# Moving the third and fourth output store of each batch from ScalarE's queue to SyncE's

## The chip, the cores and the metric

The kernel runs on one core of a Trainium2 chip. The time is device microseconds of a whole execution; lower is better. A profiled execution also gives a span from the first to the last instruction, some 1.7 us less than the time. Ratios are the mean time of one kernel's fast runs over that of the other's of the same rounds, so they are not quite the ratio of the medians that are quoted; a run is called slow when it is over 1.5% above the fastest of the same kernel. "First scores" below is the start of a batch's first score matmul, and a batch is measured from its first scores to the next batch's.

## The reference

Causal attention with 16 extra "beacon" keys that every query sees, then a gated feed-forward block:

```python
scores = q @ concat(beacon_k, k).T / 8          # B, H, S, D = 8, 8, 576, 64
scores = where(causal, -1e9, scores)
x = softmax(scores) @ concat(beacon_v, v)       # -> 4608 tokens x 512
out = (gelu(x @ w_gate) * (x @ w_val)) @ w_out  # d_ff = 1536, result float32
```

## The kernel before

A pass of the batch loop (b = 1 to 7) does, interleaved on TensorE, the output matmuls of feed-forward chunk b-1 (`o(n)` issues n of 48), the scores and attention of batch b, and then the gate and value matmuls of chunk b. The output leaves in four stores of 256 KB each. Attention outputs are turned by DMA transposes on SyncE (`turn_dma`), and so are the q and k of batch b+1 (`transpose_dma`, ten of them). GpSimd issues the loads of batch b+2.

```python
def store(engine):
    for out_ap, in_ap in stores:
        keep(engine.dma_start(out=out_ap, in_=in_ap))
    stores.clear()
...
            turn_dma(b, 2)
            o(6)
            av(b, 3)
            o(7)
            store(nc.scalar)          # third store of the batch
            turn(b, 3)
            put(b, 3)
            o(4)
            keep(nc.scalar.preload_act_table_set(SET_GELU))
            for kk in (0, 3, 1, 2):
                for fi in range(2):
                    gv_mms(b, fi, kk, last=kk == 2)     # Gelus 0 and 1
        for fi in range(F_TILES):
            if fi >= 2:
                gate_val(b, fi, ...)                    # matmuls, Gelu, product
            ...
            if fi == 0:
                store(nc.scalar)      # fourth store: behind Gelus 0 and 1 on ScalarE
                if b and b + 1 < B:
                    hold(b, 2)
                    load_v(b + 1)
                if b and b + 2 < B:
                    load_qk(b + 2)
                if 2 <= b + 1 < B:
                    transpose_dma(b + 1)
```

Three PSUM buffers (the pool `psum_s`) are shared by the scores and by the gate and value results.

The softmax here doesn't subtract the row's maximum and nothing guards it: scores larger than these inputs give would overflow.

## Time and profile before

| | before |
|---|---|
| time, first three runs | 372.77, 375.12, 615.39 us (the last a lone outlier) |
| profiled span, mean granted TensorE clock | 371.4 us, 0.999 |
| TensorE, ScalarE busy | 361.0, 187.1 us |
| stores on ScalarE, on SyncE | 28 of 256 KB, 9 (the last two chunks) |

The page, the waits, one batch of the timeline and the windows batch by batch are shown and read in the prediction. In the waits, a line is "who waits, for whom: us in total, times, longest". In the timeline, a line is start, length, engine, source line, operation, operands, and in brackets the idle time just before it with what ended it; SPq and ACTq are instructions that only issue a DMA. In the windows, a line is the stretch, its length, then busy time (and instruction count) of TensorE's matmuls and weight loads, VectorE, ScalarE and GpSimd, then granted clock, DMA share and GB/s.

### The profile page before, as it was taken

How to read it: one execution, taken by the hardware profiler on the slowest of the kernel's cores; microseconds unless marked ns; L12 is line 12 of the kernel's file. 1: busy time of each engine (PE TensorE's matmuls, PEld its weight loads, DVE VectorE, ACT ScalarE, POOL GpSimd, SP SyncE). 2: the span in 40 equal slices, each digit the busy share in tenths (PEclk: the TensorE clock that was granted, in tenths of full speed). 3: DMA queues.
4: the chain of work that ended last, by engine and by line, in shares of the span. 5: the costliest groups of instructions: out<-in, count | busy, mean ns of one | idle time of the engine just before them, and what ended most of it. 6: DMA issues, size and time to landing. Idle time of an engine off the chain costs nothing.

```text
span 371.4 us, 7554 instructions
## 1 busy us (share of the span) xinstructions
PE 361.0 (97%) x3061; PEld 182.6 (49%) x3061; DVE 151.5 (41%) x277; ACT 187.1 (50%) x243; POOL 160.5 (43%) x288
## 2 busy tenths in 40 slices
PE   7899999999998999999989999999999999999996
PEld 6664446444643455444634454445534464444443
DVE  4554545332533334433524253434444353424332
ACT  3963587238823593349623882369324963331210
POOL 8834486574548152944384453835320430000000
PEclk9999999999999999999999999999999999999999
DMA  8999999899179924999399936992491040000103
GB/s 109 178 204 205 192 131 145 103 158 139 50 114 170 125 66 92 142 152 75 98 120 148 124 52 111 174 128 75 94 165 30 28 112 29 0 2 28 56 34 111
DMA packets 154900, 39.65 MB, mean 107 GB/s; under 512 B 141424, under 2 KB 150384, under 8 KB 154864
## 3 DMA queue, kind: packets, MB, share of 16 engines
q0 software_dynamic: 104848, 19.11, 72.1%
q1 hardware_dynamic: 45984, 12.71, 21.7%
q10 hardware_dynamic: 4032, 7.34, 6.3%
q8 instruction: 24, 0.39, 0.5%
q14 instruction: 12, 0.10, 0.1%
HBM read 38.27 MB, written 9.44 MB: 128 GB/s over the span
## 4 chain that ended last, share of the span: by engine, by line
PE 85%; DMA 5%; SPq 4%; DVE 3%; ACT 1%; issue 1%; ACTq 0%
PE gv_ps L172 38%; PE o_ps L172 24%; PE x_ps L172 9%; PE s_ps L172 8%; DMA qkT<-q_sb 5%; SPq L238 3%; PE t_ps L180 2%; PE v_ps L172 2%; PE g_ps L172 2%; DVE qkT L217 1%; PE w_ps L172 1%; SPq L368 1%; DVE hT_sb L427 1%; DVE y_sb L336 1%; ACT ge_sb L175 1%
## 5 line engine op out<-in xcount | busy, mean ns | idle before, releaser
L175 ACT ACTIVATE ge_sb<-gv_ps 128x512 bf16<-128x512 f32 x101 | 58.5, 597 | 139.3 <-PE gv_ps L172 124.3
L427 DVE TENSOR_TENSOR hT_sb<-gv_ps,ge_sb 128x512 bf16<-128x512 f32 x101 | 68.2, 690 | 120.7 <-ACT ge_sb L175 120.6
L172 PE MATMUL gv_ps<-xT_sb,wg_sb 128*128 128x512 bf16 x404 | 111.6, 379 | 3.5 <-DVE hT_sb L427 3.5
L172 PE MATMUL gv_ps<-xT_sb,wv_sb 128*128 128x512 bf16 x404 | 111.5, 379 | 0.0
L172 PE MATMUL o_ps<-wo_sb,hT_sb 128*128 128x512 bf16 (+2 forms) x444 | 106.7, 374 | 0.0
L175 ACT ACTIVATE expT<-s_ps 128x960 bf16<-128x960 f32 (+3 forms) x112 | 99.7, 967 | 7.9 <-PE s_ps L172 7.5
L298 POOL TENSOR_SCALAR_AFFINE_SELECT expT<-expT 128x256 bf16<-128x256 bf16 (+2 forms) x140 | 51.5, 385 | 65.5 <-ACT expT L175 64.9
L172 PEld LDWEIGHTS <-wg_sb 128*128 128x128 bf16 x432 | 42.0, 98 | 54.8 <-issue 4.9
L172 PEld LDWEIGHTS <-wv_sb 128*128 128x128 bf16 x432 | 42.2, 98 | 50.5
L172 PEld LDWEIGHTS <-hT_sb 128*128 128x128 bf16 x444 | 38.8, 97 | 42.3 <-DVE y_sb L336 3.1
L172 PEld LDWEIGHTS <-expT 128*128 128x128 bf16 (+1 forms) x960 | 33.5, 97 | 11.0 <-DVE y_sb L336 4.3
L172 PE MATMUL x_ps<-v_sb,expT 128*128 128x65 bf16 (+1 forms) x960 | 37.1, 193 | 0.0
L108 POOL DMA_DIRECT2D v_sb<-in_v_dram x40 | 33.7, 860 | 5.9 <-DMA wv_sb<-in_moe_w_val_dram 1.7
L172 PE MATMUL s_ps<-qkT 64*128 64x512 bf16 (+5 forms) x384 | 33.5, 281 | 2.5 <-DVE qkT L221 1.6
L446 DVE COPY o_sb<-o_ps 128x512 f32<-128x512 f32 (+2 forms) x37 | 25.0, 676 | 26.6 <-PE o_ps L172 25.4
L108 POOL DMA_DIRECT2D k_sb<-in_k_dram x30 | 25.2, 842 | 20.0 <-DMA q_sb<-in_q_dram 13.6
L336 DVE TENSOR_TENSOR y_sb<-x_ps,r_sb 128x320 bf16<-128x320 f32 (+1 forms) x47 | 28.8, 612 | 1.6
L334 DVE RECIPROCAL r_sb<-x_ps 128x5 f32<-128x5 f32 (+1 forms) x47 | 9.6, 204 | 47.1 <-PE x_ps L172 47.1
L108 POOL DMA_DIRECT2D q_sb<-in_q_dram x30 | 25.4, 885 | 4.4 <-DMA wo_sb<-in_moe_w_out_dram 3.5
L172 PEld LDWEIGHTS <-qkT 64*128 64x128 bf16 x384 | 14.3, 94 | 19.3 <-issue 11.0
L378 POOL COPY hold_sb<-xT_sb 128x2 bf16<-128x2 bf16 x6 | 1.1, 185 | 34.1 <-DMA xT_sb<-y_sb 34.1
L613 ACT ACT_TABLE_LOAD x7 | 9.0, 1283 | 10.8 <-DVE o_sb L446 10.8
(49 smaller groups left out, 118.8 us busy)
## 6 DMA issues: line engine op xcount, KB each, us to landing
out_dram<-o_sb ACTq DMA_DIRECT2D x28, 256.0 KB, 3.0
v_sb<-in_v_dram POOLq DMA_DIRECT2D x24, 128.0 KB, 6.4
q_sb<-in_q_dram POOLq DMA_DIRECT2D x24, 128.0 KB, 9.2
k_sb<-in_k_dram POOLq DMA_DIRECT2D x18, 128.0 KB, 7.7
out_dram<-o_sb SPq DMA_DIRECT2D x7, 256.0 KB, 2.0
wo_sb<-in_moe_w_out_dram POOLq DMA_DIRECT2D x3, 512.0 KB, 14.4
wg_sb<-in_moe_w_gate_dram POOLq DMA_DIRECT2D x2, 512.0 KB, 11.1
wv_sb<-in_moe_w_val_dram POOLq DMA_DIRECT2D x2, 512.0 KB, 12.7
```

The lines of the kernel that those rows point to most:

```text
L108: keep(nc.gpsimd.dma_start(out=out_ap, in_=in_ap))
L172: keep(nc.tensor.matmul(out_ap, lhsT, rhs, start=start, stop=stop, **kw))
L175: keep(nc.scalar.activation(out_ap, in_ap, func, **kw))
L180: keep(nc.tensor.transpose(out_ap, in_ap, ident[0:n, 0:n]))
L217: keep(nc.vector.tensor_copy(out_ap, in_ap))
L238: nc.sync.dma_start_transpose(out=qkT[:, :, w, c + j * P : c + j * P + n], in_=src[0:n, j, :, :].rearrange("p h d -> p (h d)"),)
L298: nc.gpsimd.affine_select(out=d, in_=d, pattern=[[0, 2], [1, n]], compare_op=ALU.is_ge, fill=0.0, base=NB if t == 0 else 0, channel_multip ...
L334: keep(nc.vector.reciprocal(r, x[:, :, :, D:DV]))
L336: nc.vector.tensor_tensor(out=y_of[i][:, :, h0:h1, :].rearrange("p j b d -> p b j d"), in0=x[:, :, :, 0:D], in1=r.to_broadcast([P, h1 - h0 ...
L427: nc.vector.tensor_tensor(out=h_of[ci][:, fi, :], in0=gv_of.pop((ci, fi))[1], in1=ge_sb, op=ALU.mult)
L446: keep(nc.vector.tensor_copy(o_sb[:, ti, c0:c1], o_ps))
L613: keep(nc.scalar.preload_act_table_set(SET_GELU))
```

## The change

The third and fourth store of each batch are issued on SyncE's queue again, behind the turns. The intent is to free ScalarE's queue.

```diff
             av(b, 3)
             o(7)
-            store(nc.scalar)
+            store(nc.sync)
             turn(b, 3)
...
             if fi == 0:
-                store(nc.scalar)
+                store(nc.sync)
                 if b and b + 1 < B:
                     hold(b, 2)
```

## The prediction

> **What bounds the kernel now.** I read the page first, then the waits, then one batch of the timeline, then the batches side by side.
>
> ```profile
> span 371.4 us, 7554 instructions
> PE 361.0 (97%) x3061; PEld 182.6 (49%) x3061; DVE 151.5 (41%) x277; ACT 187.1 (50%) x243; POOL 160.5 (43%) x288
> ...
> PE 85%; DMA 5%; SPq 4%; DVE 3%; ACT 1%; issue 1%; ACTq 0%
> ...
> out_dram<-o_sb ACTq DMA_DIRECT2D x28, 256.0 KB, 3.0
> ```
>
> TensorE is busy for 361.0 of 371.4 us, so no change that leaves its work alone can win more than 10.4 us (2.8%), and some of that is the start. ScalarE is half idle: taking 14 of its 28 store issues away (0.34 us each in the trace, 4.8 us in all) is worth nothing as work. What counts is where a store on ScalarE's in-order queue waits. The table of waits shows it:
>
> ```profile
> ACT ge_sb L175 <- DMA qkT<-q_sb: 14.9, 4, 4.4
> ...
> ACT L613 <- DVE o_sb L446: 10.8, 7, 1.6
> ...
> PE gv_ps L172 <- DVE hT_sb L427: 3.5, 4, 1.4
> ```
>
> A Gelu has no reason to wait for a DMA transpose of the next batch's q. The timeline of the second pass of the batch loop (b = 2) explains it; these are rows of it:
>
> ```profile
> 102.08 0.37 ACTq L454 DMA_DIRECT2D out_dram<-o_sb  x1
> ...
> 105.17 0.69 DVE L446 COPY o_sb<-o_ps 128x512 f32<-128x512 f32 x1 [0.41 <-PE o_ps L172]
> ...
> 105.66 1.21 SPq L238 DMA_TRANSPOSE qkT<-q_sb  x1
> ...
> 108.26 1.22 SPq L238 DMA_TRANSPOSE qkT<-q_sb  x1
> ...
> 113.31 0.34 ACTq L454 DMA_DIRECT2D out_dram<-o_sb  x1
> ...
> 113.75 1.57 ACT L175 ACTIVATE ge_sb<-gv_ps 128x512 bf16<-128x512 f32 x3 [4.42 <-DMA qkT<-q_sb]
> ...
> 115.12 1.02 PE L172 MATMUL gv_ps<-xT_sb,wg_sb 128*128 128x512 bf16 x4 [1.36 <-DVE hT_sb L427]
> ```
>
> The fourth store's data were copied by 105.86, but it issues only at 113.31. In the built program it waits on two semaphores: VectorE's, and one of eight that the hardware DMAs take in turn. The earlier user of that one is the second q transpose, issued at 108.26, landed at 113.23. Behind the store stand the Gelus; they come late, VectorE's product comes late, no score buffer is free, and TensorE stands for 1.36 us. Now the batches side by side, in windows from one batch's first output matmul to the next's:
>
> ```profile
> 86.53:127.37 40.84, 39.48 (x319) 19.42 (x317) 16.08 (x29) 21.90 (x29) 21.50 (x39) 1.00 1.30 116
> 127.37:166.83 39.46, 39.46 (x318) 19.43 (x317) 16.17 (x29) 22.00 (x29) 21.22 (x38) 1.00 1.21 115
> 166.83:207.42 40.59, 39.48 (x318) 19.43 (x317) 16.08 (x29) 21.89 (x29) 21.21 (x38) 1.00 1.30 113
> 207.42:247.06 39.64, 39.48 (x319) 19.40 (x317) 16.14 (x29) 22.01 (x29) 21.22 (x38) 1.00 1.26 116
> ```
>
> The second column is the length, the third TensorE's busy time. The work is 39.47 us each time; batches 2 and 4 (and 6) are over a microsecond longer than 3 and 5. The four idle gaps before such Gelu-released matmuls are 1.36 (b=2), 1.11 (b=4), 0.16 (b=5) and 0.91 us (b=6): 3.54 us. This is what the change can win.
>
> **What the Trainium skill says.** "DMA: Bandwidth & Descriptors", section "Issuing engines are not separate DMA queues": DMAs started by ScalarE, SyncE or GpSimd run on the same 16 engines and interleave, so the choice of issuer saves only the issuer's own time. The trace agrees for the bytes, but the cost here is a wait in the issuer's queue (4.4 us), not the 0.34 us of issuing. The same page, "Queues, rings and completion order": SP and ACT each have one ring on each engine, descriptors are consumed in ring order, and an engine takes packets from its rows in rotation. So stores put ahead of transposes in SyncE's ring hold those back, while in ScalarE's ring they shared. In the trace before, SyncE's transposes land in the order of issue, which fits; a store between transposes in that ring is not seen. "Perfetto Trace Analysis", section "DMA Instruction — HWDGE (DVE, Sync)": the profiled window of such a DMA starts once its semaphores are satisfied and leaves out the data movement. The case agrees: the blocked store shows 0.34 us, and its 7.4 us of waiting show only as others' idle time.
>
> **The change, part by part.** TensorE, VectorE and GpSimd keep their instruction lists exactly; ScalarE loses 14 DMAs (two for each of b = 1 to 7), SyncE gains them, both placed after the six turn transposes of the batch and before the ten transposes of the next.
>
> 1. Store three leaves ScalarE, which now waits 1.5 us for it before the table load (10.8 us over seven). ScalarE next works when a first gate matmul group is done (108.25, over 4 us after the load ends). Worth 0.
>
> 2. Store four leaves ScalarE. Its wait goes, so the 3.54 us of TensorE idle go: -3.54. In the new program the two stores wait on semaphores of DMAs eight places earlier, long landed by then, and no Gelu stands behind them.
>
> 3. SyncE's transposes start later. In b = 2 SyncE ends its last turn at 105.56 and starts the first q at 105.66. Now it issues store three (0.34, ready since 102.05) and store four (0.34, data ready at 105.86): estimated 105.65 to 106.41, so q moves to about 106.5: +0.85 us. In odd batches SyncE is free earlier (b = 3: 145.36, copy ends 146.69), so it waits for the copy: q at about 147.15 instead of 145.47, +1.7; but that q issue took 1.98 us instead of the usual 1.21, and if this slow issue does not recur just later, the second transpose moves by 0.9 only.
>
> 4. The stores' bytes change place. One store's packets took 13 us of engine time (6.3% of 16 x 371.4 us over 28 stores), 0.83 us on all 16. Before, store four moved in the midst of the GpSimd loads and the transposes (landed 119.90, and for that microsecond the transposes' ring moved almost nothing). Now it moves near 107, before those loads' packets begin (109). That gives the last transposes back about 0.85. Store three moves from an idle time into one with few transposes: no more than what item 3 counted.
>
> Net for the last transpose's landing: even batches about 0 to +0.4, odd 0 to +0.9. What does it cost? The next batch's scores need the last k transpose about 1.4 us after their batch starts (four output matmuls, 0.86, and some 0.5 into the first scores). Slack before: 1.0 (b=1: landed 86.89, batch at 86.53), 1.3 (b=2: 127.43, 127.37), 0.7 (b=3: 167.50, 166.83), 1.6 (b=4: 207.16, 207.42), 0.2 (b=5: 248.21, 247.06), and 7 in b=6, where no loads run (281.69, 287.44). Removing the stall brings the scores forward by just that stall, so the slack left is 1.0, 0, 0.7, 0.5, 0 and 6. I charge 0.3 in b = 2 and 0.5 in b = 5, and 0.2 over the rest: +1.0 of new waits at the scores.
>
> Sum: -3.54 + 1.0 = -2.5 us on the profiled execution.
>
> **Rivals.** (a) The transposes become the bound. For: slack is nearly nothing in b = 2 and 5, and the last transposes land 7 to 9 us after issue, so a late start sits in front of a crowded stretch. If the delay at the end were 2 us in each of b = 1 to 5, the waits would be 1 + 2 + 1.3 + 1.5 + 2 = 7.8 and the time 4.3 us longer, about 377.5. Against: the last four transposes are limited by shared DMA engines, from which store four is taken away. (b) A free win: if transposes land no later at all, the whole 3.5 us come, about 369.5. For it: b = 6 surely wins its 0.91. (c) Nothing: the waits at the scores eat just what the Gelu stall gave, since both hang on the same DMA engines; 373. I hold this for likelier than (a). (d) Mixing plain copies with transposes in a ring slows the transposes' issue; some issues take 2.0 to 2.5 us already, for a reason the profile does not show. Two more of those in each of six batches would delay as in (a).
>
> **Range and chances.** The three timed runs are 372.77, 375.12 and an outlier of 615.39; the profiled run was 373.12. I take 373.2 as what an undisturbed run gives, not the median. 373.2 - 2.5 = 370.7, and I add 0.5 because medians of few runs lie above the quiet ones: 371.2. Low end 368.8 (all of 3.5 won, and a little), high end 376.5 (most of rival a, or a disturbed median). Over 2% faster would need 7.5 us below 375.12, twice the idle time that the change can reach: 0.03. Over 2% slower needs rival (a) at twice my worst case: 0.03.
>
> **What would show it.** Right: no ScalarE wait on the q transposes; TensorE's idle before the Gelu-released matmuls gone; batches 2, 4 and 6 near 39.5 us; the first q of each batch at SyncE 0.8 to 1.7 us later against the last turn; the last k transposes landing within 1 us of where they did from the batch's start. Wrong: TensorE or its weight loads waiting for the k transposes by over 1 us in several batches (item 4 failed), or a stall that stays although the store has gone (item 2 failed), for instance because the Gelus wait for something that the store's wait hid.

## The result

The changed kernel takes 368.98 us (median of four, 368.65 to 369.70); before, 374.05 in the same comparison, or 372.77 to 375.12 without the outlier. The ratio of the fast runs is 0.9878 (0.9832 to 0.9925): 1.2% less. The profiled span fell from 371.4 to 367.4 us. The page of the changed kernel (span; busy time by engine; the chain that ended last; issues of the stores with size and us to landing):

```profile
span 367.4 us, 7507 instructions
...
PE 356.8 (97%) x3018; PEld 182.4 (50%) x3061; DVE 152.4 (41%) x277; ACT 188.3 (51%) x243; POOL 160.7 (44%) x288
...
PE 74%; DMA 13%; SPq 4%; POOL 3%; issue 2%; DVE 2%; ACT 1%; POOLq 0%; DVEq 0%
...
out_dram<-o_sb SPq DMA_DIRECT2D x21, 256.0 KB, 2.4
out_dram<-o_sb ACTq DMA_DIRECT2D x14, 256.0 KB, 2.8
```

TensorE's busy time is no measure of the gain: 43 matmul records are missing from this trace. The chain runs more through DMA here (13% against 5%), but that is no sign of a new bound: in the two repeats below the share is 2% and 7%. The waits of the changed kernel:

```profile
ACT ge_sb L175 <- PE gv_ps L172: 143.1, 89, 6.5
...
PEld L172 <- DMA qkT<-k_sb: 1.6, 4, 0.4
...
PEld L172 <- DMA xT_sb<-y_sb: 1.5, 3, 0.8
```

The 14.9 us that Gelus waited for q transposes, and TensorE's 3.5 us behind them, are no longer in the table; Gelus wait for matmuls only. What is left on TensorE are small waits for k transposes and for turns. The same stretch of the timeline (b = 2):

```profile
104.77 1.00 SPq L454 DMA_DIRECT2D out_dram<-o_sb  x2
105.87 1.21 SPq L238 DMA_TRANSPOSE qkT<-q_sb  x1
...
107.55 1.08 ACT L175 ACTIVATE ge_sb<-gv_ps 128x512 bf16<-128x512 f32 x2 [6.01 <-PE gv_ps L172]
...
109.70 0.60 ACT L175 ACTIVATE ge_sb<-gv_ps 128x512 bf16<-128x512 f32 x1 [1.07 <-PE gv_ps L172]
```

Both stores go out on SyncE in one go, and the third Gelu starts 1.07 us after the second ends, with its matmuls, instead of 4.42 us after it. And the batches side by side, b = 2 to 5:

```profile
85.83:125.14 39.31, 38.94 (x314) 19.48 (x317) 16.27 (x29) 22.11 (x29) 21.24 (x38) 1.00 1.22 115
125.14:165.16 40.02, 39.20 (x314) 19.41 (x317) 16.27 (x29) 22.12 (x29) 20.50 (x37) 1.00 1.23 115
165.16:204.48 39.32, 38.95 (x314) 19.57 (x317) 16.27 (x29) 22.11 (x29) 21.98 (x39) 1.00 1.30 116
204.48:244.13 39.65, 39.19 (x314) 19.44 (x317) 16.27 (x29) 22.11 (x29) 21.24 (x38) 1.00 1.22 120
```

A batch without any wait is 39.32 us, not 39.47. The long batches before (2, 4) are at that floor; batches 3 and 5 have new waits. From the two traces, first scores to first scores:

| us | start | b=1 | b=2 | b=3 | b=4 | b=5 | b=6 | rest |
|---|---|---|---|---|---|---|---|---|
| before | 46.90 | 40.42 | 40.84 | 39.46 | 40.59 | 39.64 | 40.38 | 83.17 |
| after | 46.37 | 40.26 | 39.32 | 40.02 | 39.32 | 39.65 | 39.32 | 83.18 |

Batches 2 and 4 gain 2.79 us, batch 6 gains 1.06, batch 3 loses 0.56. The 0.53 us at the start is chance: in another profile of the changed kernel the start is 46.87.

### The profile page after: what moved, and what is told of

Same layout as the page of the kernel before. It is cut to its first block, busy times and chain, and to the rows that moved or that the text cites.

```text
span 367.4 us, 7507 instructions
## 1 busy us (share of the span) xinstructions
PE 356.8 (97%) x3018; PEld 182.4 (50%) x3061; DVE 152.4 (41%) x277; ACT 188.3 (51%) x243; POOL 160.7 (44%) x288
## 2 busy tenths in 40 slices
DMA packets 154900, 39.65 MB, mean 108 GB/s; under 512 B 141424, under 2 KB 150384, under 8 KB 154864
## 4 chain that ended last, share of the span: by engine, by line
PE 74%; DMA 13%; SPq 4%; POOL 3%; issue 2%; DVE 2%; ACT 1%; POOLq 0%; DVEq 0%
PE gv_ps L172 32%; PE o_ps L172 23%; PE x_ps L172 9%; PE s_ps L172 7%; DMA qkT<-k_sb 7%; DMA q_sb<-in_q_dram 4%; SPq L238 3%; DMA qk<-in_q_dram 2%; POOL v_sb L108 2%; DMA xT_sb<-y_sb 1%; PE v_ps L172 1%; ACT expT L175 1%; PE t_ps L180 1%; PE g_ps L172 1%; POOL qk L108 1%
## 5 line engine op out<-in xcount | busy, mean ns | idle before, releaser
L175 ACT ACTIVATE ge_sb<-gv_ps 128x512 bf16<-128x512 f32 x101 | 59.5, 597 | 145.1 <-PE gv_ps L172 143.1
L427 DVE TENSOR_TENSOR hT_sb<-gv_ps,ge_sb 128x512 bf16<-128x512 f32 x101 | 69.1, 691 | 116.0 <-ACT ge_sb L175 116.0
L172 PE MATMUL o_ps<-wo_sb,hT_sb 128*128 128x512 bf16 (+2 forms) x415 | 101.7, 373 | 1.4 <-issue 0.2
```

The lines of the kernel that those rows point to most:

```text
L172: keep(nc.tensor.matmul(out_ap, lhsT, rhs, start=start, stop=stop, **kw))
L175: keep(nc.scalar.activation(out_ap, in_ap, func, **kw))
L427: nc.vector.tensor_tensor(out=h_of[ci][:, fi, :], in0=gv_of.pop((ci, fi))[1], in1=ge_sb, op=ALU.mult)
```

## The experiments

Theory **W**: the gain is the end of one wait. On ScalarE, Gelus stand behind the fourth store, and that store waits for the semaphore that a q transpose of the next batch used before it. What is lost again comes from transposes that now start later. Rival **Q**: ScalarE's queue is relieved of issues and of waits for copies, third store as much as fourth. Rival **T**: the bytes leave the crowded stretch and go ahead of it. All kernels below gave correct results.

**The changed kernel again** (run twice), as a yardstick.

> The changed kernel again, as the yardstick on this chip for the three others: about 369.0 us, ratio to before about 0.988 (seen: 0.9878), profiled span 367.4 within 0.5.

> The changed kernel once more beside the next three: 368.6 to 369.4 us, ratio to before 0.988.

Measured: 369.36 us, ratio 0.9883 (0.9842 to 0.9924), and 369.58 us, ratio 0.9883 (0.9852 to 0.9913). The place of the new waits changes: batch 3 was 39.31 and batch 5 39.96 us in the first of these profiles, 39.72 and 39.91 in the second. Their sum over b = 2 to 6, above 39.32, is 0.6 to 1.0 us in the three profiles.

**Only the fourth store on SyncE.**

```diff
             if fi == 0:
-                store(nc.scalar)
+                store(nc.sync)
```

> Only the fourth store goes to SyncE; the third stays on ScalarE with its 1.5 us wait before the table load. Theory W (the gain is the end of the Gelus' wait behind the fourth store's DMA semaphore): all of the gain, 369.0 us or up to 0.5 less because SyncE has one issue less ahead of the transposes; no Gelu waits for a q transpose. Rival Q (the gain is ScalarE's queue being relieved, third store as much as fourth): about half of the gain, 371 us. Rival T (bytes moved out of the crowded stretch): also about 369.

Measured: 369.52 us, ratio 0.9888 (0.9844 to 0.9932). All the gain is there with the third store, and its 1.5 us wait before the table load, still on ScalarE. Q would have had half. W holds, though the median is half a microsecond above its 368.5 to 369.0: in the profile no Gelu waits for a q transpose, and batches 2 to 6 are 39.32 us long but for one of 39.62. (That profiled run, 371.11 us, lost some 2 us at its start, in 6.83 us at half the clock.) T is not touched.

**Only the third store on SyncE.**

```diff
             o(7)
-            store(nc.scalar)
+            store(nc.sync)
             turn(b, 3)
```

> Only the third store goes to SyncE, ahead of the transposes; the fourth stays on ScalarE behind the second Gelu, and the built program still has it wait for the second q transpose. Theory W (the gain is the end of that wait): no gain; the transpose starts some 0.4 us later, so the stalls stay or grow a little: 373 to 375 us. Rival Q (ScalarE's queue relieved): half of the gain, 371.

Measured: 382.12 us, ratio 1.0202 (1.0119 to 1.0284), slower, by more than W said; whether it is slower by over 2% is unclear. Its profile (a slow execution at granted clock 0.991; the fast ones had 0.991 and 0.995) shows where:

```profile
ACT ge_sb L175 <- DMA qkT<-q_sb: 21.3, 4, 5.6
...
PE gv_ps L172 <- DVE hT_sb L427: 12.6, 6, 2.6
```

Now all six batches b = 1 to 6 stall. This run gives a scale. With t the issue of the fourth store after the batch's first scores, and the idle time of TensorE that follows (b = 1 is left out: its batch has other work in it, 40.26 us without a stall against 39.32):

| | b=2 | b=3 | b=4 | b=5 | b=6 |
|---|---|---|---|---|---|
| before: t, idle | 25.98, 1.36 | 24.61, 0 | 25.74, 1.11 | 24.77, 0.16 | 25.53, 0.91 |
| third only: t, idle | 26.81, 2.19 | 26.36, 2.03 | 26.13, 1.50 | 26.68, 2.06 | 27.19, 2.57 |

In eight of the nine stalls, idle is t - 24.62 within 0.01 us (26.36 is the exception, by 0.29). TensorE pays for each microsecond by which that store is late, one for one; W's reading is that this begins once the three result buffers are full. The store was later because the transpose it waits for was: SyncE did the third store first. W missed two things. It allowed 0.4 us for this delay, but after the first scores the second q transpose was issued 0.1 to 1.3 us later than before and landed 0.4 to 3.2 us later, so the idle time grew from 3.5 to 12.6 us. And in two stretches of 3.41 us after a stall the granted clock was 0.5.

**The fourth store ahead of the table load and of all Gelus, on ScalarE.** Bytes, copy and the semaphore waited for are unchanged.

```diff
             o(4)
+            store(nc.scalar)
             keep(nc.scalar.preload_act_table_set(SET_GELU))
```

> The fourth store on ScalarE is moved ahead of the table load and the first Gelus; its bytes, semaphore and copy are the same, and it still waits for the second q transpose. W: now all Gelus stand behind it, and with three score buffers TensorE stops after the third gate/value group: some 5 to 6 us more idle in each of batches 1 to 6 than with no wait, so 395 to 405 us. Q and rival T (bytes and their time decide): no change, 373, since the same issues and bytes are at nearly the same place.

Measured: 415.51 us, ratio 1.1115 (two runs). The timeline of b = 2 in its profile, the stores' merged row first:

```profile
108.12 11.23 ACTq L454 DMA_DIRECT2D out_dram<-o_sb  x2
...
119.38 1.28 ACT L614 ACT_TABLE_LOAD   x1 [12.41 <-DMA qkT<-q_sb]
...
122.04 1.86 PE L172 MATMUL gv_ps<-xT_sb,wg_sb 128*128 128x512 bf16 x4 [5.70 <-DVE hT_sb L427]
```

The idle time of TensorE is 4.0 to 6.4 us a batch and 31.3 us in all, as W said; Q and T said no change. The rest is again the clock, seen in the windows of this run:

```profile
113.00:120.00 7.00, 3.34 (x16) 1.41 (x15) 0.00 (x0) 0.62 (x1) 6.70 (x10) 1.00 1.39 124
120.00:127.00 7.00, 4.96 (x13) 1.76 (x13) 2.58 (x4) 2.83 (x5) 5.08 (x7) 0.52 1.94 170
127.00:134.00 7.00, 7.00 (x34) 3.19 (x33) 2.24 (x4) 2.39 (x4) 1.95 (x3) 1.00 2.55 146
```

The clock column falls to 0.52 after the stall and returns. Over the run it was at half for 34.1 us in six stretches of 3.41 or 6.83 us, which, as an estimate, costs up to half of that, 17 us: 367 + 31 + 17 is 415, against a span of 412.5, since part of a half-clock stretch is idle time anyway (120 to 122 here).

**The fourth store later, behind the sixth Gelu, still on ScalarE.**

```diff
-            if fi == 0:
+            if fi == 5:
                 store(nc.scalar)
+            if fi == 0:
                 if b and b + 1 < B:
```

> Both stores stay on ScalarE; the fourth is issued behind the sixth Gelu instead of behind the second, so that the q transpose whose semaphore it waits for has landed by then. W: the Gelu stalls go as in the changed kernel though ScalarE keeps all its issues: 368.5 to 369.5 us; TensorE's idle of 1.36, 1.11, 0.16 and 0.91 us is gone, and SyncE starts its first q transpose as early as before. Q: no gain, 373. T: the bytes move later into the crowd, so no gain or worse, 373 to 375, with TensorE waiting for k transposes.

Measured: 369.01 us, ratio 0.9883 (0.984 to 0.9925), with all stores on ScalarE. ScalarE in its b = 2:

```profile
113.87 0.60 ACT L175 ACTIVATE ge_sb<-gv_ps 128x512 bf16<-128x512 f32 x1 [1.13 <-PE gv_ps L172]
115.60 0.60 ACT L175 ACTIVATE ge_sb<-gv_ps 128x512 bf16<-128x512 f32 x1 [1.13 <-PE gv_ps L172]
115.61 0.35 ACTq L454 DMA_DIRECT2D out_dram<-o_sb  x1
117.33 0.60 ACT L175 ACTIVATE ge_sb<-gv_ps 128x512 bf16<-128x512 f32 x1 [1.13 <-PE gv_ps L172]
```

The store issues beside a running Gelu, and none waits. The store's bytes go into the crowd (it lands 35.3 to 37.3 us after the first scores in b = 2 to 5, against 30 to 33 before). Q and T fall for the main part of the gain: neither the queue nor the bytes had to move.

**Both stores on SyncE, behind the ten transposes** (run twice).

```diff
             o(7)
-            store(nc.sync)
             turn(b, 3)
...
             if fi == 0:
-                store(nc.sync)
...
                 if 2 <= b + 1 < B:
                     transpose_dma(b + 1)
+                store(nc.sync)
```

> Both stores on SyncE but behind the ten transposes of the next batch instead of ahead. W: the whole gain stays, and the small waits that the late transposes made (0.3 to 0.5 us in batches 2 to 4) go: 368.0 to 369.0 us. Q: as the changed kernel, 369. T: the gain came from moving the bytes ahead of the crowd, so it goes: 372 to 374.

> Both stores on SyncE behind the transposes, repeated beside the changed kernel. Theory W with late transposes (the changed kernel gives back about 1 us by waits for late transposes, which this one does not have): 0.3 to 1 us under the changed kernel in this call, and its batches 2 to 6 all 39.31 to 39.40 us long from first scores to first scores. Rival: the 0.7 us difference of the medians seen before is noise of the chip; then no difference, and one of the batches 2 to 5 at 39.6 or more in this one too.

Measured: 368.64 us, ratio 0.9866 (0.9827 to 0.9906), and 368.99 us, ratio 0.9885 (0.985 to 0.9919). The second run's batches 2 to 5:

```profile
86.35:125.67 39.32, 38.95 (x314) 19.41 (x317) 16.27 (x29) 22.11 (x29) 21.22 (x38) 1.00 1.17 112
125.67:164.99 39.32, 38.95 (x314) 19.38 (x317) 16.26 (x29) 22.11 (x29) 21.21 (x38) 1.00 1.20 118
164.99:204.31 39.32, 38.95 (x314) 19.45 (x317) 16.27 (x29) 22.11 (x29) 21.21 (x38) 1.00 1.19 109
204.31:243.62 39.31, 38.94 (x314) 19.41 (x317) 16.26 (x29) 22.11 (x29) 21.22 (x38) 1.00 1.14 127
```

All are at the floor, in both profiles (39.31 to 39.38), and in none of the changed kernel's three: the waits that came back are those of the late transposes. In the first profile the last k transpose of b = 2 to 5 landed 1.3 to 2.6 us earlier after the first scores than in the changed kernel's. In times the step is small: the ten runs at clock 0.999 or 1.0 have a mean of 368.8 us against 369.4 for the changed kernel's twelve, two more (370.67, 370.95) had a clock of 0.99, and the ratios to before overlap. It is the best of the kernels tried, by about 0.2%, which the intervals do not separate.

**All four stores on SyncE.** Every `store(nc.scalar)` becomes `store(nc.sync)`.

> All four stores on SyncE, the first two ahead of the turn transposes. Theory W: nothing more is to be won, since stores one and two make no Gelu wait; they delay the turns by their issue (0.34 us) at most and the turns have slack: 368.5 to 369.5 us. Rival Q (ScalarE's queue relieved is what pays): another 2 us less, 367.

Measured: 370.27 us, ratio 0.9903 (0.9861 to 0.9945): 0.8 us above W's estimate, and away from Q's. Batches 3 and 5 are 40.66 and 39.89 us; aligned with the kernel that has the stores behind, weight loads of the scores start 1.33 and 0.74 us late, after waits for k transposes. The early stores on SyncE do cost something, then; how they delay these transposes was not taken apart.

**More warm-up matmuls**, to test a surprise (below).

```diff
-    warm(66)
+    warm(98)
```

> The changed kernel with 32 more warm-up matmuls at the start (64 instructions of TensorE), for one look at the slow landings of turn transposes. If a 16 KB packet on the instruction queue (one per 256 TensorE instructions) is what makes a turn land in 4 us or more instead of 2.3 to 2.5, the packets come some 3 us earlier against the batch, the last turns of b = 3 and 5 land in 2.3 to 2.7 us, and other turns near the packets land in 3 us or more. If the slow ones are bound to their place in the program, the last turns of b = 3 and 5 stay at 4 us or more. Time: 1 to 2 us over the changed kernel, as the warm-up is longer.

Measured: 369.62 us, ratio 0.9889 (two runs). The last turn transposes of b = 3 and 5 landed in 2.49 and 2.47 us, and others in 3 us or more. The extra warm-up cost nothing: it lay beside the wait for the first loads (first scores at 7.59 us against 7.53).

## Why the prediction was right

1. **The bound.** "What counts is where a store on ScalarE's in-order queue waits": confirmed by the late store (no move, all the gain), by the early one (46 us more than the changed kernel), and by the straight line of idle time against the store's issue. One reading was off: of the fourth store's 7.4 us between copy and issue, only the last 4.0 were its wait at the head of the queue. Until 109.34 it stood behind the second Gelu.

2. **Item 1, the third store is worth 0.** Confirmed: left on ScalarE it costs nothing that the noise would show (369.52 against 369.36 us).

3. **Item 2, -3.54 us: the mechanism was right, the size short.** This is the term that was mis-sized. Aligning the weight loads of both traces, the jumps at the four stalls are 1.52, 1.28, 0.32 and 1.07 us, 4.19 in all. The idle gaps undercount by 0.16 each: a matmul is drawn 379 ns long, but in an undisturbed row the next one starts some 215 ns after it, and a gap is counted only from the end of the drawn bar. The 1.36 us of idle in b = 2 therefore are 1.36 + 0.379 - 0.215 = 1.52 us lost, just the jump. Four such corrections are 0.65 us, the whole difference between 3.54 and 4.19.

4. **Item 3, later transposes.** Predicted +0.85 in even batches and +0.9 to +1.7 in odd ones; measured after the first scores +0.91, +0.92 and +1.42 (b = 2, 4, 6) and +2.1, +2.7 and +1.9 (b = 1, 3, 5). The odd ones were under-sized: a slow issue (1.08 us for a store in b = 3) came on top of the copy's wait.

5. **Item 4, the last transpose's landing.** Predicted 0 to +0.4 in even batches and 0 to +0.9 in odd; measured +0.09 and +0.58 (b = 2, 4), and +0.71, +1.27 and -0.86 (b = 1, 3, 5). The late store lands in the crowd and still wins all, so these bytes matter less than item 4 assumed. The order that the prediction had not seen is seen now: stores and transposes on SyncE landed in the order of issue in every profile (b = 2 of the changed kernel: stores at 20.3 and 21.1 us after the first scores, the first q behind them at 22.5).

6. **The +1.0 us of new waits.** 1.03 us in this trace (0.70 in b = 3, 0.33 in b = 5 above the floor of 39.32), so right in sum, but by luck: I charged b = 2 and 5; b = 2 has no wait in any of the three profiles, and the two repeats have 0.63 and 0.99. Only part is at the scores. Of the 0.70, aligned with the kernel that has the stores behind, some 0.4 came at the gate matmuls, which waited for the last turn of that batch.

Sum for the span: the floor shows 4.31 us of excess before and 1.03 after in b = 2 to 6, plus 0.16 in b = 1 and 0.53 of chance at the start: -3.97, or -3.44 without the chance, against -2.5. The half microsecond that I added for medians of few runs was not there. The time of 368.98 lies in the range, at its low end.

Of the rivals, (a) and (c) did not come: the new waits are 1 us in all, where they needed 8 and 4. Rival (b) gave nearly the measured time (369.5 against 368.98), but for a wrong reason: it left the new waits out and, as I did, counted the stall short. Rival (d) did not come either: SyncE's slow transpose issues (1.75 us or more) are 11 before and 5 after the change. I wrote that the profile does not show their reason; the last section has what most of them go with.

One thing stays argued: the semaphore could not be changed alone, as the framework hands it out and the wait cannot be dropped without another order of DMAs. What is shown is that the store is released when that transpose lands, that it does not use the transpose's data, and that in another place, with no late wait, it costs nothing. In the packed traces the two carry the same semaphore number in every batch (110 in b = 2; eight numbers recur in turn), and in 17 of the 18 batches (b = 1 to 6) of the kernel before, the third-only and the early one, the fourth store issues 0.08 us after that transpose lands. In the late kernel it issues 2.2 to 3.8 us after.

## What to carry to other kernels

A DMA that an engine issues can hold up that engine's compute by a wait that is not in the source: here a semaphore shared in turn by hardware DMAs, so that a store waited for the eighth DMA before it. Where a compute instruction is released by a transfer that it does not use, look at the DMA issue just ahead of it in its queue, and move that issue to where its semaphore is long free; either another queue or a later place in the same queue will do. Then look at what the moved issue stands in front of: behind the urgent transposes it cost nothing, ahead of them about 1 us.

## What the Trainium skill lacked or had wrong

- "DMA: Bandwidth & Descriptors", section "Issuing engines are not separate DMA queues", says that the choice of issuer saves only the issuer's time. It lacks that the issuer's queue may stand behind a semaphore wait of the DMA: a 0.34 us issue held ScalarE for 4.4 us and TensorE for 1.5 us (b = 2), and the choice of place was worth 1.2%.
- "Runtime: NRT & Kernel Launch", section "Instruction fetch mechanics", calls the cost of crossing a 16 KiB block (256 instructions) "mostly hidden". It lacks what the fetch does to other DMAs. The fetches show in the trace as 24 packets of 16 KB on the instruction queue, 0.9 to 1.7 us each in the kernel before, for 6122 matmuls and weight loads. Here they are not hidden from DMA transposes. In the eleven profiles of kernels with the same TensorE program, the last of a batch's six turn transposes landed in 2.45 to 2.50 us where no such packet ran meanwhile (33 cases) and in 3.82 to 4.70 us where one did (33 cases). With 64 more TensorE instructions the packets moved: the last ones of all six batches (b = 2 to 7) landed in 2.46 to 2.49 us, and the fifth of the six, which no packet met in the eleven profiles (2.22 to 2.62 us), took 3.00 to 3.17 us in the three cases where one now did. The slow issues go with the packets too: in all twelve profiles 82 of the 150 transpose issues on SyncE that met a packet took 1.75 us or more, and 17 of the other 1074. That they are caused by it was not tested. The window of the kernel before in which the last turn of b = 3 is slow has the packet in its queue lines (queue, packets, MB, share):

```profile
q8 instruction: 1, 0.02, 1.2%
```

- "TensorE: Matmul & The Clock Gate", section "Why this matters for your kernels", asks for no idle gaps over about 3 us. In the profile of the third store alone on SyncE the clock fell to half after idle gaps of 2.23 and 2.06 us (2.4 and 2.2 with the 0.16 that the drawn bars hide), though not after others of 2.57 and 2.19. Counted in windows of 3.41 us from where that trace's clock records begin, the first two gaps lie each in one window; the other two are cut by a window's edge, with at most 1.87 us in one. That is not the whole rule: the profile of the fourth store alone on SyncE fell to half at 10.4 us, after a window with 1.3 us of idle time in all. The half-clock stretches of 3.41 us, and of 6.83, fit the window length of 3413 ns which the section "Part 1: The HAM clock gate" gives.
- No page says that the idle time which the profile shows before a matmul is short by the overhang of the drawn bar: here 0.16 us for a gap after a 512-column matmul (379 ns drawn, 215 ns of pace).
